# Attention, expert layer and feed-forward in one kernel: 33 slots outside any condition, one conditional block for the rest, later tile loads and decoding

## The chip, the cores and the metric

The kernel runs on one core of a Trainium2 chip. The core's engines are TensorE (PE, matrix multiplication), VectorE (DVE), ScalarE (ACT), GpSimd (POOL) and SyncE (SP, which here issues nearly all DMA). Each engine works through its own list of instructions in order and waits on semaphores for the others. The metric is the device time of one execution in microseconds (us); less is better. A measurement of this kernel can tell a change from none at about 0.3%, some 5 us.

## What is computed

Three layers follow one another on 4608 tokens of 512 values.

```python
x = attention(q, k, v, phi)                  # 8 batches x 8 heads, 576 positions, 64 values a head
idx = argmax(logits(x, expert_emb)); gate = softmax(...)[idx]
for e in range(8):                           # each token goes to one of 8 experts
    out[idx == e] = gate * (relu(x[idx == e] @ w1[e]) @ w2[e])      # 512 -> 1024 -> 512
h = out @ w_in                               # 512 -> 2048
y = (h * sigmoid(1.702 * h)) @ w_out         # 2048 -> 512
```

`w_in` and `w_out` come as 64-bit floats. [...] Every product is made of three 16-bit matmuls (high times high, high times low, low times high).

## The kernel before

**Expert layer.** Tokens are sorted by expert into slots of 128 rows. Four early slots run beside the end of the attention. Then `Moe.run` goes over slots 0 to 31 (`ALWAYS` = 32), which run whatever the data are. How many slots there are in all depends on the data (a table entry that `reg(2, 0)` loads into a register); with these inputs slot 32 is the last. `Moe.slot` lists the work of one slot with a time for each piece and writes it in the order of those times: the first layer of slot s (`product`, `relu`), the second layer of slot s - 1 (`second`, `measure`, `leave`), the input of slot s + 2 (`take`: scale, split, a DMA transpose into `xT`), the gather for slot s + 5, and, under a condition (`when`), the change of weights when the expert changes.

**Feed-forward.** A tile is 256 sorted tokens; there are 18. `FF` is done in two passes of 1024 hidden values, so there are 36 tile visits q, each of two halves h = 2q (first layer, line 1466, which ends in tanh and two elementwise steps) and h = 2q + 1 (second layer, line 1509). From slot 20 (`ALONE`) each slot carries one half in its middle: slot 20 + h carries half h. After the slots, `Ffn.run` does the other halves alone. `Ffn.load` brings a tile's input by SP: two DMA transposes into `x2T` (line 1447), `x2s` and `x2i`; there are two buffers. It is called in an even half, for the tile after it.

**Slots behind 31, before.** `Ffn.run` begins with half 12 and puts slot 32 and up to five more behind one half each: `swap` (weights), a conditional `alone` (the whole slot, line 1555) and `ahead` (gather and `take` of later slots, unconditional). Slots from 38 on stand in one last conditional block, `rest` (line 1561), behind half 18.

**Decoding.** `Weights.pieces` is a list of small steps; a slot or half issues some of them between its own work (`share`). The weights of the first pass are decoded in slots 0 to 18, those of the second pass from slot 20 on, 4 pieces in an even slot and 16 in the next, then 24 per tile in `Ffn.run`. The first step of a block of weights is `low`, an ACT instruction (line 1288) that reads the raw words a DMA has brought (`raw`, line 1262). `Weights.more` issues those DMAs as buffers come free. `widen` adds three more buffers in room that the dispatch tables had used, and fetches into them at once.

**Conditions.** A `tc.If` makes every engine that has work inside it load and compare the register. Where the block is skipped, the engine waits for its own earlier work and DMAs and then counts up its semaphores by what the block would have added. Whatever comes later and needs another engine's work from inside the block also waits until that engine has passed the condition.

Of the kernel before, what the change touches and what calls it, by code (L numbers as in the profile page):

```python
# [23 lines left out]
NT, DM, E, FE, FF = 4608, 512, 8, 1024, 2048  # L24
P = 128
PB = 96
NC = 6
XW = 514
YI, YS, YW = 2 * DM, 2 * DM + 2, 2 * DM + 4
HEAD = 8  # L30
EARLY = 4
ALWAYS = NT // P - EARLY
MORE = 6
ALONE = 20
HF = FF // 2
TILES = NT // (2 * P)
SHARE = 4, 16
# [10 lines left out]
def do(pieces):  # L48
    for f in pieces:
        f()  # L50
# [749 lines left out]
class Moe:  # L800
# [302 lines left out]
        if self.other:  # L1103
            self.other.pop(0)()

    def ahead(self, s):

        end = ALWAYS + MORE
        if s + 2 < end:
            do(self.take(s + 2))  # L1110
        if s + 5 < end:
            self.gather(s + 5)

    def slot(self, s, share, ffn):

        ev, end, h = [], ALWAYS + MORE, 0.65
        TR, TLO, TS, TL, TLH, TT, TG, TM, TQ, TQ1 = TIMES

        def add(t, fs, dt=0.0):
            ev.extend((t + i * dt, len(ev) + i, f) for i, f in enumerate(fs))  # L1120

        def begins(r, *fs):
            def f():
                with self.when(r):  # L1124
                    for x in fs:
                        x()
            return f

        def change(k, r):
            return lambda: self.change(k, r)  # L1130

        def bound(k):
            return lambda: self.bound(k)

        add(0, [lambda a=a, fi=fi: self.product(s, a, fi) for a in range(2) for fi in range(4)], h)
        for a in range(2):
            add(4 * h * (a + 1) + TR, self.relu(s, a), TLO)
        if s + 1 < ALWAYS:
            add(8 * h + (5 if ffn else 0), [begins(s + 1, change(0, s + 1))])
        y = 8 * h + 0.02  # L1140
        if ffn:
            add(y, ffn, 5.2)
            y += 10.4
        if s:
            add(y, [lambda k=k: self.second(s - 1, k) for k in range(8)], h)
            y += 8 * h
            m = self.measure(s - 1)
            add(y, m[:1])
            add(y, [begins(s, change(1, s))])

            add(TQ, [begins(s - 1, bound(0))] if s > 1 else [])
            add(TQ1, [begins(s - 2, bound(1))] if s > 2 else [])
        add(TM, self.later, TS)
        self.later = m[1:] if s else []
        c = self.leave(s - 2)
        add(TL, c[:1])
        add(TL + TLH, c[1:], TLO)
        if s + 2 < end:
            add(TT, self.take(s + 2), TLO)
        if s + 5 < end:  # L1160
            add(TG, [lambda: self.gather(s + 5)])
        add(0.2, share, (20 if ffn else 10.2) / max(len(share), 1))
        for _, _, f in sorted(ev, key=lambda e: e[:2]):
            f()

    def run(self, ffn):

        n, self.later = len(self.other), []
        for s in range(ALWAYS):
            left = n * (ALONE - 2 - s) // (ALONE - 1)  # L1170
            share = []
            while len(self.other) > max(left, 0):
                share.append(self.other.pop(0))
            if s == ALONE - 1:
                ffn.open()
            if s >= ALONE:
                share = ffn.share(SHARE[(s - ALONE) % 2])
            self.slot(s, share, [lambda part=part: ffn.half(s - ALONE, part) for part in range(2)] if s >= ALONE else [])
        do(self.later + self.leave(s - 1))
        self.layer2(s)  # L1180
        with self.when(s):
            self.bound(0)
            self.bound(1)
        with self.when(s - 1):
            self.bound(1)

    def layer2(self, s):
        for k in range(8):
# [22 lines left out]
    def rest(self):  # L1211

        g = self.g
        for s in range(ALWAYS + MORE, g.ns):
            with g.tc.If(self.reg(2, 0) > s):
                self.swap(s)
                self.bounds(s)
                self.gather(s)
                do(self.take(s))
                self.alone(s)  # L1220


class Weights:
# [129 lines left out]

        return [high, low]

    def pieces(self):
        n, none = self.n, [lambda: None]
        exact = self.exact
        dec = [none * 8 if exact else self.decode(k, i) for k in range(2) for i in range(n)]
        out = []  # L1360

        def at(q, j, k0, k1):
            if k0 * n <= q < k1 * n:
                out.append(dec[q][j])

        def fetch(q):
            if q < 2 * n and exact:
                out.append(lambda: self.fetch(*divmod(q, n)))

        def put(k, i, j):  # L1370
            if k and i < n:
                out.append(self.put(0, i)[j])

        fetch(0)
        fetch(1)
        out.append(self.more if not exact else lambda: None)
        at(0, 0, 0, 1)
        for k in range(2):
            if k:
                for i in range(3):  # L1380
                    for j in range(2):
                        put(k, i, j)
                at(n, 0, 1, 2)
            for i in range(n + LAG):
                q = k * n + i
                put(k, i + 3, 0)
                at(q, 1, k, k + 1)
                at(q - 1, 6, k, k + 1)
                at(q, 2, k, k + 1)
                if self.nlf > 2:  # L1390
                    at(q + 1, 0, k, k + 1)
                put(k, i + 3, 1)
                at(q, 3, k, k + 1)
                at(q - 1, 7, k, k + 1)
                if self.nlf < 3:
                    at(q + 1, 0, k, k + 1)
                at(q, 4, k, k + 1)
                at(q, 5, k, k + 1)
                if i < n:
                    fetch(q + 2)  # L1400
                w = 1024 // self.N
                if i < n and i % w == w - 1:
                    out.append(lambda k=k, j=i // w: self.square(k, j))
                if i > n:
                    out += none
            r, f = self.settle(k)
            out += none * 2 + [r] + none * 4 + [f]
        p = [self.put(1, i) for i in range(n)]
        for i in range(n + 1):
            out += ([p[i][0]] if i < n else []) + ([p[i - 1][1]] if i else [])  # L1410
        return out


class Ffn:
# [108 lines left out]
    def half(self, h, part, n=0):  # L1523

        q = h // 2
        if h % 2:
            self.layer2(q, part, n)
        else:
            if part == 0:
                if q == TILES:  # L1530
                    self.factors(1)
                if q + 1 < 2 * TILES:
                    self.load(q + 1)
            elif q >= TILES:
                self.room2(q)
            self.layer1(q, range(4 * part, 4 * part + 4))
            if part:
                self.after(self.x[q], 0)

    def run(self):  # L1540

        g, moe = self.g, self.moe
        s, end = ALWAYS, ALWAYS + MORE
        moe.swap(s)
        for h in range(ALWAYS - ALONE, 4 * TILES):
            if h == 2 * TILES:
                do(self.share(len(self.other)))
            for part in range(2):
                self.half(h, part, 3)
            if h == ALWAYS - ALONE:  # L1550
                do(moe.leave(ALWAYS - 1))
            if ALWAYS < s <= end:
                moe.bounds(s - 1)
            if s < end:
                with g.tc.If(moe.reg(2, 0) > s):
                    moe.alone(s)
                if s + 1 < end:
                    moe.swap(s + 1)
                moe.ahead(s)
            elif s == end:  # L1560
                with g.tc.If(moe.reg(2, 0) > s):  # L1561
                    moe.rest()
            s += 1


@with_exitstack
def tile_kernel(ctx, tc, q, k, v, phi, emb, tau, w1, w2, w_in, w_out, out):
    nc = tc.nc
    g = Obj()
# [23 lines left out]
    moe = Moe(g, ctx.enter_context(tc.tile_pool(name="w", bufs=1)))  # L1593
    g.xp = ctx.enter_context(tc.tile_pool(name="xp", bufs=1))
    g.psa = ctx.enter_context(tc.tile_pool(name="psa", bufs=1, space=PSUM))
    with tc.manual_schedule():
        at, aq, wst, wsr = ExitStack(), ExitStack(), ExitStack(), ExitStack()
# [18 lines left out]

        attention(g, moe, second)
        at.close()
        g.weights.widen(wsr.enter_context(tc.tile_pool(name="wsr", bufs=1, side="right", reuse_waits="tile")))

        def third():
            wsr.close()
            wst.close()
            g.fp = ctx.enter_context(tc.tile_pool(name="fp", bufs=2, reuse_waits="tile"))
            p = ctx.enter_context(tc.tile_pool(name="wst2", bufs=1, reuse_waits="tile"))
            return Weights(g, 1, p, moe.junk, DM // 2, 2).pieces()

        ffn = Ffn(g, moe, third)
        moe.run(ffn)
# [31 lines left out]
```

## Time and profile before

| what | value |
|---|---|
| time, median of 3 runs (lowest, highest) | 1538.82 us (1536.34, 1541.42) |
| time of the profiled execution | 1532.62 us |
| its span, first to last instruction | 1530.7 us |
| PE busy | 1373.3 us, 90% |
| DVE busy | 886.1 us, 58% |
| ACT busy | 697.7 us, 46% |
| POOL busy | 274.8 us, 18% |
| mean granted TensorE clock | 0.952 of full speed |

The profiled execution took 1.92 us more than its span. Busy times are sums over the whole span; where an engine waited has to be read from stretches of it.

### The profile page before, as it was taken

How to read it: one execution, taken by the hardware profiler on the slowest of the kernel's cores; microseconds unless marked ns; L12 is line 12 of the kernel's file. 1: busy time of each engine (PE TensorE's matmuls, PEld its weight loads, DVE VectorE, ACT ScalarE, POOL GpSimd, SP SyncE). 2: the span in 40 equal slices, each digit the busy share in tenths (PEclk: the TensorE clock that was granted, in tenths of full speed). 3: DMA queues.
4: the chain of work that ended last, by engine and by line, in shares of the span. 5: the costliest groups of instructions: out<-in, count | busy, mean ns of one | idle time of the engine just before them, and what ended most of it. 6: DMA issues, size and time to landing. Idle time of an engine off the chain costs nothing. (4 is left out here: it accounts for less than half of the span.)

```text
span 1530.7 us, 31869 instructions
## 1 busy us (share of the span) xinstructions
PE 1373.3 (90%) x11632; PEld 963.4 (63%) x11632; DVE 886.1 (58%) x2232; ACT 697.7 (46%) x1655; POOL 274.8 (18%) x301
## 2 busy tenths in 40 slices
PE   4989877878789886989999988899999999999997
PEld 4767656556557555666667645566666666666664
DVE  3887995866456543465564455676545554445553
ACT  2767864444645542355564344354533332223331
POOL 2543430442122210111011011111000011110011
PEclk9987888989899998999999999999999999999999
DMA  9999933798785875564343454233214323333321
GB/s 214 240 231 260 248 88 96 171 169 145 117 92 96 137 63 93 87 155 99 74 67 88 74 82 89 60 95 77 53 51 105 83 75 89 77 83 90 84 73 42
DMA packets 229809, 168.87 MB, mean 110 GB/s; under 512 B 149338, under 2 KB 199130, under 8 KB 229602
## 3 DMA queue, kind: packets, MB, share of 16 engines
q1 hardware_dynamic: 223362, 145.85, 46.0%
q0 software_dynamic: 6240, 20.50, 6.8%
q8 instruction: 101, 1.65, 0.6%
q14 instruction: 106, 0.87, 0.4%
HBM read 96.60 MB, written 39.82 MB: 89 GB/s over the span
## 5 line engine op out<-in xcount | busy, mean ns | idle before, releaser
L1509 PE MATMUL op<-wo,gt 128*128 128x512 f16 x1728 | 386.2, 383 | 18.3 <-DVEq L1561 5.9
L1466 PE MATMUL hp<-x2T,wi 128*128 128x256 f16 x3456 | 387.1, 274 | 17.2 <-DVE th L1480 12.1
L1466 PEld LDWEIGHTS <-wi 128*128 128x128 f16 x3456 | 338.6, 98 | 66.5 <-issue 20.0
L1509 PEld LDWEIGHTS <-gt 128*128 128x128 f16 x1728 | 170.3, 99 | 220.3 <-issue 16.7
L1471 ACT ACTIVATE th<-th,fk 128x256 f32<-128x256 f32 x288 | 145.9, 508 | 342.0 <-DVE th L1470 340.7
L985 PE MATMUL hp<-xT,wh 128*128 128x128 f16 x3552 | 214.1, 223 | 32.3 <-ACTq L1124 9.1
L985 PEld LDWEIGHTS <-wh 128*128 128x128 f16 x3552 | 208.2, 100 | 46.7 <-issue 32.3
L1010 PE MATMUL yp<-wh,hT 128*128 128x512 f16 x888 | 204.7, 388 | 14.4 <-PEq L1124 8.0
L1470 DVE TENSOR_TENSOR th<-hp,x2s 128x256 f32<-128x256 f32 x288 | 122.1, 424 | 157.1 <-PE hp L1466 152.9
L1010 PEld LDWEIGHTS <-hT 128*128 128x128 f16 x888 | 86.9, 100 | 120.5 <-PEq L1124 12.7
L1480 DVE SCALAR_TENSOR_TENSOR th<-th,hp 128x256 f32<-128x256 f32 x288 | 118.7, 412 | 16.5 <-ACT th L1471 16.4
L1490 DVE SCALAR_TENSOR_TENSOR gt<-th,gt 128x256 f16<-128x256 f32 x288 | 121.1, 420 | 6.3 <-ACT gt L1482 3.5
L1482 ACT ACTIVATE gt<-th 128x256 f16<-128x256 f32 x288 | 115.9, 402 | 7.8 <-DVE th L1480 7.5
L1516 POOL DMA_INDIRECT out_dram<-o,x2i x36 | 35.4, 984 | 427.2 <-DVE o L1515 427.2
L1515 DVE SCALAR_TENSOR_TENSOR o<-op,x2f,o 128x512 f32<-128x512 f32 x36 | 27.0, 751 | 126.3 <-PE op L1509 126.3
L1309 POOL TENSOR_TENSOR dlf<-dlf,raw 128x256 f32<-128x256 f32 (+1 forms) x48 | 46.5, 970 | 240.3 <-DVE raw L1305 101.6
L1001 DVE SCALAR_TENSOR_TENSOR hT<-hp,hT 128x512 f16<-128x512 f32 x74 | 50.7, 687 | 66.1 <-ACT hT L998 47.4
L956 POOL DMA_INDIRECT xg<-xbuf,idx x38 | 40.0, 1052 | 272.6 <-DVE hT L1001 135.1
L1520 ACT ACTIVATE o<-op,x2f 128x512 f32<-128x512 f32 x36 | 24.7, 686 | 112.9 <-PE op L1509 111.7
L370 PE MATMUL xp<-bdv,aT 128*96 128x264 f32 x192 | 65.9, 454 | 9.7 <-ACT xh L376 4.9
L998 ACT ACTIVATE hT<-hp 128x512 f16<-128x512 f32 x74 | 43.5, 589 | 61.1 <-PE hp L985 59.7
L971 DVE SCALAR_TENSOR_TENSOR x<-xg,x 128x512 f16<-128x512 f32 x42 | 37.7, 898 | 50.3 <-ACT x L966 48.7
(250 smaller groups left out, 1460.2 us busy)
## 6 DMA issues: line engine op xcount, KB each, us to landing
wr<-in_moe_w_dram SPq DMA_DIRECT2D x40, 512.0 KB
xbuf<-xh SPq DMA_DIRECT2D x18, 576.0 KB
yb<-y SPq DMA_DIRECT2D x37, 257.0 KB
qr<-in_q_dram SPq DMA_DIRECT2D x16, 576.0 KB
kv<-in_k_dram SPq DMA_DIRECT2D x16, 576.0 KB
kv<-in_v_dram SPq DMA_DIRECT2D x16, 576.0 KB
part<-o SPq DMA_DIRECT2D x36, 256.0 KB
o<-part SPq DMA_DIRECT2D x36, 256.0 KB
```

The source lines that it names most:

```text
L370: nc.tensor.matmul(t[:PB], lhsT=self.aT[:, c], rhs=self.bdv, start=True, stop=True)
L985: self.g.nc.tensor.matmul(o.hp[a][:, fi], lhsT=self.wh[0][f // 2][:, ta, k, f % 2 * P:f % 2 * P + P], rhs=o.xT[:, 4 * tb + k], start=(n == ...
L1001: nc.vector.scalar_tensor_tensor(out=part(1), in0=o.hp[a], scalar=0.0, in1=part(0), op0=ALU.max, op1=ALU.subtract)
L1010: self.g.nc.tensor.matmul(o.yp, lhsT=o.hT[:, ta, k], rhs=self.wh[1][k // 2][:, tb, k % 2], start=(k + i == 0), stop=(k + i == 9))
L1309: nc.gpsimd.tensor_tensor(out=o.lf, in0=o.lf, in1=o.lo.bitcast(F32), op=ALU.mult)
L1466: nc.tensor.matmul(x.hp, lhsT=w.wi[:, ta, k, a * P:(a + 1) * P], rhs=o.xT[:, 4 * tb + k].rearrange("p j q -> p (j q)"), start=(i == 0), st ...
L1470: nc.vector.tensor_tensor(out=x.th, in0=x.hp, in1=o.s, op=ALU.mult)
L1471: nc.scalar.activation(out=x.th, in_=x.th, func=AF.Tanh, scale=k2[:, 0:1])
L1480: nc.vector.scalar_tensor_tensor(out=x.th, in0=x.th, scalar=1.0, in1=x.hp, op0=ALU.add, op1=ALU.mult)
L1482: nc.scalar.activation(out=o.gt[-1][:, 0], in_=x.th, func=AF.Copy, scale=2.0**-GS)
L1490: self.g.nc.vector.scalar_tensor_tensor(out=o.gt[i][:, 1], in0=o.th[i], scalar=2.0**-GS, in1=o.gt[i][:, 0], op0=ALU.mult, op1=ALU.subtract)
L1509: nc.tensor.matmul(op, lhsT=o.gt[a][:, ta, j * P:(j + 1) * P], rhs=w.wo[:, a, tb], start=(i == 0), stop=(i == 23))
```

## The change

- `ALWAYS` is 33, so slot 32 is written like the slots ahead of it and carries half 12. `Ffn.run` begins with half 13. `ahead` and the five conditional slots behind single halves are gone, and so are their unconditional gathers and `take`s.
- All slots from 33 on stand in one condition, `rest`, which is issued in half 13 between its two parts. The conditional `bound`s that ended `Moe.run` go into it.
- `Ffn.load(q + 1)` is no longer in half 2q, in the middle of slot 20 + 2q, but at the head of slot 21 + 2q. The tile is used in half 2q + 2 as before.
- In the second pass 20 empty pieces stand behind the first fetch. With 4 and 16 pieces a slot, decoding starts in slot 22 and not in slot 20.
- `widen` is called in slot 1, at time 6 of the slot's list, and not ahead of slot 0.

```diff
 NC = 6
 XW = 514
 YI, YS, YW = 2 * DM, 2 * DM + 2, 2 * DM + 4
+WIDE = 1
 HEAD = 8
 EARLY = 4
-ALWAYS = NT // P - EARLY
-MORE = 6
+ALWAYS = NT // P - EARLY + 1
 ALONE = 20
 HF = FF // 2
 TILES = NT // (2 * P)
...
         if self.other:
             self.other.pop(0)()

-    def ahead(self, s):
-
-        end = ALWAYS + MORE
-        if s + 2 < end:
-            do(self.take(s + 2))
-        if s + 5 < end:
-            self.gather(s + 5)
-
     def slot(self, s, share, ffn):

-        ev, end, h = [], ALWAYS + MORE, 0.65
+        ev, end, h = [], ALWAYS, 0.65
         TR, TLO, TS, TL, TLH, TT, TG, TM, TQ, TQ1 = TIMES

         def add(t, fs, dt=0.0):
...
             add(TT, self.take(s + 2), TLO)
         if s + 5 < end:
             add(TG, [lambda: self.gather(s + 5)])
+        if s == WIDE:
+            add(6, [self.widen])
         add(0.2, share, (20 if ffn else 10.2) / max(len(share), 1))
         for _, _, f in sorted(ev, key=lambda e: e[:2]):
             f()
...
                 ffn.open()
             if s >= ALONE:
                 share = ffn.share(SHARE[(s - ALONE) % 2])
+
+                if (s - ALONE) % 2:
+                    ffn.load((s - ALONE) // 2 + 1)
             self.slot(s, share, [lambda part=part: ffn.half(s - ALONE, part) for part in range(2)] if s >= ALONE else [])
         do(self.later + self.leave(s - 1))
         self.layer2(s)
-        with self.when(s):
-            self.bound(0)
-            self.bound(1)
-        with self.when(s - 1):
-            self.bound(1)

     def layer2(self, s):
         for k in range(8):
...
     def rest(self):

         g = self.g
-        for s in range(ALWAYS + MORE, g.ns):
-            with g.tc.If(self.reg(2, 0) > s):
-                self.swap(s)
-                self.bounds(s)
-                self.gather(s)
-                do(self.take(s))
-                self.alone(s)
+        self.reg(2, 0)
+        with g.tc.If(self.reg(2, 0) > ALWAYS):
+            with self.when(ALWAYS - 1):
+                self.bound(0)
+                self.bound(1)
+            with self.when(ALWAYS - 2):
+                self.bound(1)
+            for s in range(ALWAYS, g.ns):
+                with g.tc.If(self.reg(2, 0) > s):
+                    self.swap(s)
+                    self.bounds(s)
+                    self.gather(s)
+                    do(self.take(s))
+                    self.alone(s)


 class Weights:
...

         return [high, low]

-    def pieces(self):
+    def pieces(self, wait=0):
+
         n, none = self.n, [lambda: None]
         exact = self.exact
         dec = [none * 8 if exact else self.decode(k, i) for k in range(2) for i in range(n)]
...
         fetch(0)
         fetch(1)
         out.append(self.more if not exact else lambda: None)
+        out += wait * none
         at(0, 0, 0, 1)
         for k in range(2):
             if k:
...
             if part == 0:
                 if q == TILES:
                     self.factors(1)
-                if q + 1 < 2 * TILES:
+                if ALWAYS - ALONE <= h and q + 1 < 2 * TILES:
                     self.load(q + 1)
             elif q >= TILES:
                 self.room2(q)
...

     def run(self):

-        g, moe = self.g, self.moe
-        s, end = ALWAYS, ALWAYS + MORE
-        moe.swap(s)
-        for h in range(ALWAYS - ALONE, 4 * TILES):
+        moe, first = self.moe, ALWAYS - ALONE
+        for h in range(first, 4 * TILES):
             if h == 2 * TILES:
                 do(self.share(len(self.other)))
             for part in range(2):
+                if h == first and part == 0:
+                    self.load(h // 2 + 1)
                 self.half(h, part, 3)
-            if h == ALWAYS - ALONE:
-                do(moe.leave(ALWAYS - 1))
-            if ALWAYS < s <= end:
-                moe.bounds(s - 1)
-            if s < end:
-                with g.tc.If(moe.reg(2, 0) > s):
-                    moe.alone(s)
-                if s + 1 < end:
-                    moe.swap(s + 1)
-                moe.ahead(s)
-            elif s == end:
-                with g.tc.If(moe.reg(2, 0) > s):
+                if h == first and part == 0:
+                    do(moe.leave(ALWAYS - 1))
                     moe.rest()
-            s += 1


 @with_exitstack
...

         attention(g, moe, second)
         at.close()
-        g.weights.widen(wsr.enter_context(tc.tile_pool(name="wsr", bufs=1, side="right", reuse_waits="tile")))
+        wide = wsr.enter_context(tc.tile_pool(name="wsr", bufs=1, side="right", reuse_waits="tile"))
+        moe.widen = lambda: g.weights.widen(wide)

         def third():
             wsr.close()
             wst.close()
             g.fp = ctx.enter_context(tc.tile_pool(name="fp", bufs=2, reuse_waits="tile"))
             p = ctx.enter_context(tc.tile_pool(name="wst2", bufs=1, reuse_waits="tile"))
-            return Weights(g, 1, p, moe.junk, DM // 2, 2).pieces()
+            return Weights(g, 1, p, moe.junk, DM // 2, 2).pieces(sum(SHARE))

         ffn = Ffn(g, moe, third)
         moe.run(ffn)
```

The order of ACT's list in slot 20 before: `relu` of the slot (`hT`), then the first decoding step of the second pass (`dlf<-raw`), then the tanh (`th`) and gate (`gt`) steps of half 0.

```order
L1124 UNCONDITIONAL_BRANCH x2
L998 ACTIVATE hT<-hp 128x512
L1288 ACTIVATE dlf<-raw 128x256
L1471 ACTIVATE th<-th,fk 128x256 x2
L1482 ACTIVATE gt<-th 128x256
L1471 ACTIVATE th<-th,fk 128x256
```

And now, at the same place:

```order
L1116 UNCONDITIONAL_BRANCH x2
L998 ACTIVATE hT<-hp 128x512
L1472 ACTIVATE th<-th,fk 128x256 x2
L1483 ACTIVATE gt<-th 128x256
L1472 ACTIVATE th<-th,fk 128x256
L1483 ACTIVATE gt<-th 128x256
```

The instruction that reads `raw` has left slot 20; it stands in the same way ahead of the tanh steps of half 2, in slot 22.

SP's list now, from the end of slot 20 into slot 21: the skipped fetch of an expert's second weights (`wr`), the load of tile 1, a condition, a partial result (`part`) and the `xT` of a later slot.

```order
L846 DMA wr_142<-in_moe_w_dram 128x2x512
L920 UNCONDITIONAL_BRANCH x2
L1116 UNCONDITIONAL_BRANCH
L1448 DMA_TRANSPOSE x2T<-yb 128x8x128 x2
L1451 DMA x2s<-ys 128x256
L1453 DMA x2i<-yb 128x2x4
L1116 COMPARE_AND_BRANCH
L1116 UNCONDITIONAL_BRANCH x2
L1522 DMA part<-o 128x512
L973 DMA_TRANSPOSE xT<-x_9155 128x8x128
```

Before, the load of tile 1 stood in slot 20 itself, directly behind the three fetches of `raw` and one condition; the load has moved behind slot 20's writes of `yb` and `ys`.

DVE's list now, in half 13 between its parts: decoding steps, the two instructions that end slot 32 (`y`), then the load of the register and the condition at line 1207.

```order
L1301 SCALAR_TENSOR_TENSOR wo_3030<-raw,wo_3030 128x256
L1304 TENSOR_SCALAR raw<-wo_3030 128x256
L1290 TENSOR_SCALAR wo_3030<-raw 128x256
L1044 TENSOR_TENSOR y_13235<-ym,fac 128x1
L1050 SCALAR_TENSOR_TENSOR y_13235<-yp,yr,y_13235 128x512
L838 TENSOR_LOAD tabs
L1207 COMPARE_AND_BRANCH
L1208 COMPARE_AND_BRANCH
```

Before, the last such condition (line 1561) stood behind the last gate step of half 18; now it stands behind slot 32's last output, and behind it on TensorE comes the second part of half 13.

## Rows read from the trace of the kernel before

**Rows 1.** The page's DMA issues: names, engine, operation, count, size.
```profile
yb<-y SPq DMA_DIRECT2D x37, 257.0 KB
```

**Rows 2.** Windows: stretch, length, busy time (instructions) of each engine, granted clock, DMA share, GB/s.
```profile
573.22:609.95 36.73, 24.19 (x216) 18.38 (x217) 12.90 (x35) 10.35 (x26) 1.35 (x3) 0.81 0.60 97
...
833.76:979.28 145.52, 127.92 (x890) 80.08 (x891) 75.01 (x203) 56.22 (x131) 17.45 (x25) 0.94 0.42 75
979.28:1519.00 539.72, 539.72 (x3737) 365.57 (x3736) 289.55 (x762) 199.08 (x469) 49.06 (x55) 1.00 0.31 77
```

**Rows 3.** Timeline of PE in slot 20: start, duration, work, [idle before, what ended it].
```profile
573.22 5.52 PE L985 MATMUL hp<-xT,wh 128*128 128x128 f16 x96
578.84 5.41 PE L1466 MATMUL hp<-x2T,wi 128*128 128x256 f16 x48
596.35 8.08 PE L1466 MATMUL hp<-x2T,wi 128*128 128x256 f16 x48 [12.09 <-DVE th L1480]
...
609.95 2.23 PE L985 MATMUL hp<-xT,wh 128*128 128x128 f16 x37 [0.35 <-PEq L1124]
```

**Rows 4.** Timeline of ACT in slot 20.
```profile
595.01 0.43 ACT L1288 ACTIVATE dlf<-raw 128x256 f32<-128x256 uint32 x1 [18.31 <-DMA raw<-in_moe_w_in_dram]
```

**Rows 5.** Timeline of SP's DMA issues, end of slot 19 and slot 20.
```profile
572.97 3.80 SPq L1447 DMA_TRANSPOSE x2T<-yb  x2
...
584.36 1.29 SPq L1262 DMA_DIRECT2D raw<-in_moe_w_in_dram  x3
585.95 10.22 SPq L1447 DMA_TRANSPOSE x2T<-yb  x2
```

**Rows 6.** Timeline of PE: the starts of slots 26, 27 and 28.
```profile
723.24 5.52 PE L985 MATMUL hp<-xT,wh 128*128 128x128 f16 x96
...
745.13 5.52 PE L985 MATMUL hp<-xT,wh 128*128 128x128 f16 x96 [0.39 <-DVE raw L1305]
...
767.27 4.91 PE L985 MATMUL hp<-xT,wh 128*128 128x128 f16 x85
```

**Rows 7.** Timeline of PE from slot 31 to half 20.
```profile
833.76 5.52 PE L985 MATMUL hp<-xT,wh 128*128 128x128 f16 x96 [0.30 <-DVE th L1470]
...
855.88 5.34 PE L1010 MATMUL yp<-wh,hT 128*128 128x512 f16 x24 [1.06 <-ACTq L1124]
...
885.56 9.40 PE L1509 MATMUL op<-wo,gt 128*128 128x512 f16 x36 [2.99 <-ACT x L966]
...
911.86 12.21 PE L1509 MATMUL op<-wo,gt 128*128 128x512 f16 x48 [2.54 <-DVEq L1555]
...
967.42 12.02 PE L1509 MATMUL op<-wo,gt 128*128 128x512 f16 x48 [5.93 <-DVEq L1561]
979.28 10.64 PE L1466 MATMUL hp<-x2T,wi 128*128 128x256 f16 x96
```

**Rows 8.** Source view of line 1561: count, duration ns min/median/max, first and last start.
```profile
L1561 PEldq COMPARE_BRANCH x1: 3802/3802/3802, 959.6 to 959.6; - x1
```

**Rows 9.** Source view of line 1555, the same columns.
```profile
L1555 PEldq COMPARE_BRANCH x7: 70/342/570, 870.6 to 946.9; - x7
```

**Rows 10.** Timeline of DVE behind the condition at line 1561.
```profile
967.49 0.23 DVE L1504 TENSOR_SCALAR x2f<-x2i,fk 128x2 f32<-128x2 f32 x1 [3.57 <-DVEq L1561]
```

**Rows 11.** Timeline of ACT and DVE in slot 21: one tile output, one slot output.
```profile
620.69 0.69 ACT L1520 ACTIVATE o<-op,x2f 128x512 f32<-128x512 f32 x1 [7.26 <-PE op L1509]
...
622.46 0.69 ACT L1047 ACTIVATE y<-yp,yr 128x512 f16<-128x512 f32 x1
623.82 0.75 DVE L1050 SCALAR_TENSOR_TENSOR y<-yp,yr,y 128x512 f16<-128x512 f32 x1
```

**Rows 12.** Timeline of PE, ACT and SP in slots 0 and 1.
```profile
319.49 0.39 PE L985 MATMUL hp<-xT,wh 128*128 128x128 f16 x2 [8.69 <-ACTq L1124]
318.24 0.66 ACT L1288 ACTIVATE dlf<-raw 128x512 f32<-128x512 uint32 x1 [8.28 <-SPq L1124]
307.42 6.23 SPq L1262 DMA_DIRECT2D raw<-in_moe_w_in_dram  x4
```

## The prediction

> **What bounds the kernel now.** I read the windows first, then the timeline of PE in the two stretches that the diff touches, then who ended its waits. The chain of work that ended last shows only the final output transfers, so it does not help. From 979.28 us on PE is busy all the time at a granted clock of 1.00 [rows 2]: 52 halves in 539.72 us, 10.38 us a half. That stretch is bound by matmuls, and the diff adds and removes none there. So the end moves by what the start of half 20 moves, and that is decided ahead of it.
>
> Two stretches ahead of it lose time. [...] The stretch from slot 31 to half 20 takes 145.52 us with PE busy 127.92, clock 0.94 [rows 2]. A slot with a half in it that meets no such wait takes 745.13 - 723.24 = 21.89 us (slot 26, even) or 767.27 - 745.13 = 22.14 us (slot 27, odd) [rows 6].
>
> In slot 20 PE stands idle 12.09 us until DVE's `th` step [rows 3]. DVE is only the last link: ACT is in order, and ahead of its tanh stands the first decoding step, which waited 18.31 us for `raw` to land [rows 4]. SP issued those three fetches at 584.36 and tile 1's transposes right behind them; the latter took 10.22 us to issue, against 3.80 us for tile 0's [rows 5]. From first issue to use a fetch took 595.01 - 584.36 = 10.65 us. So a fetch is read as soon as it can be, with a tile load crowding it, on the one engine that half 0 needs.
>
> From slot 31 to half 20 the waits end on conditions and on the `take` of slots that never run: 2.99 us (ACT's `x`, line 966), 2.54 (line 1555), 5.93 (line 1561) [rows 7]. The 37 writes of `yb` are 4 early slots and slots 0 to 32 [rows 1]: slot 32 runs, and no later one does.
>
> **Slot 20.** With 20 empty pieces, 4 + 16, ACT reads `raw` in slot 22, some 44 us (two slots) after the fetch; the longest latency above is 10.65 us. The tile load no longer crowds it either. Slot 20 becomes an even slot like slot 26: 36.73 - 21.89 = 14.8 us saved. Lower bound: only the idle time goes, 12.1. Where could the stall go? The same decoding step now stands ahead of slot 22's tanh, but its data are old by then. In `Ffn.run` decoding is 16 pieces further behind: 365 pieces with the empty ones, less 124 issued in slots 20 to 32, leaves 241, and the 12 odd halves 13 to 35 take 24 each, 288. So nothing is left to be dumped at half 36. Cost there: nothing, hidden by PE, which is busy all that time while DVE is busy 289.55 of 539.72 us [rows 2].
>
> **Tile loads.** In program order `load(q + 1)` comes later, not sooner: from the middle of an even slot to the head of the next odd one. Four DMAs move past SP's `xT` and `yb` of the even slot and ahead of `part` and `xT` of the odd one. The room left is one odd slot and the first product of the next, 22.14 + 5.52 = 27.7 us. Tile 0's load was used 578.84 - 572.97 = 5.9 us after its first issue, without a wait [rows 3, 5]; the crowded one needed at least its 10.22 us. Both fit. Behind the moved issues (about 5 us of SP's time) wait `part` and an `xT` that is used two slots later. I take 0.
>
> **Slots 31 and 32, halves 12 to 19.** Now: slot 31, 22.14; slot 32 with half 12, 21.89; slot 32's second layer, 5.34 plus the 1.06 us that it waits for a condition on ACT, as slot 31's does at 855.88 [rows 7], 6.40; halves 13 to 19, 7 x 10.38 = 72.66. That is 123.1 us before the one condition that remains.
>
> That condition (line 1207) stands between the parts of half 13. TensorE's second part needs a PSUM buffer that the block's last slot would use, so it waits until DVE has passed the condition. From the end of the first part: ACT writes `o`, 0.69; ACT writes `y`, 0.69; DVE writes `y`, 0.75 [rows 11]; the register's load, which no row shows alone, for which I take the 0.34 us median of a short conditional step [rows 9]; DVE's idle time over such a condition, 3.57 [rows 10]: 6.0 us together. The old one cost PE 5.93 [rows 7]. PE's own 3.80 us over it [rows 8] runs beside that. After the old wait half 19 took 979.28 - 967.42 = 11.86 instead of 10.38 us, 1.5 for the lower clock; I take that again. Sum: 123.1 + 6.0 + 1.5 = 130.6, against 145.52: 14.9 us saved. Bounds of the wait: 3.8 (PE's own) and twice 6.0, if the skip also has to wait for SP's two writes of slot 32, which stand just ahead of it; behind SP's condition are two `raw` fetches, a `part` and tile 8, all used a half or more later.
>
> Here length could matter, since the block holds 17 slots and the old one 12. The conditions around one slot (line 1555) took PE 0.07 to 0.57 us, the one around 12 slots 3.80 [rows 8, 9]: a jump over much code costs more than one over little, but two points don't tell how it grows. If DVE's 3.57 grew with length it would be 3.57 x 17/12 = 5.06, and the whole 1.5 us dearer. [...] I stay at 6.0.
>
> **`widen`.** PE waits 8.69 us in slot 0 for ACT, and ACT 8.28 for a `raw` that it decodes [rows 12]. SP's four fetches around 307.42 to 313.65 hold that one and two of the three that `widen` adds behind it. The one that ACT waits for is issued first in either order, so removing later fetches should change nothing: 0. Bounds: the three crowd it, and all 8.7 us go; or the three, now ahead of slot 3's `xT`, delay it by up to the 10.65 us of a fetch. ACT decodes in the same order as before.
>
> **Sum.** 14.8 + 14.9 = 29.7 us. The profiled execution took 1532.62 us, 1.92 more than its span; its span becomes 1530.7 - 29.7 = 1501.0 and its time 1502.9. The median of the runs shown is 1538.82, 6.2 us above the profiled one, so on that footing I forecast 1538.82 - 29.7 = 1509 us, a ratio of 0.981.
>
> **Rivals.**
> - Slot 0's wait goes as well. For it: several transfers share the time in which ACT waits. Against it: the order of issue. 1509 - 8.7 = 1500.
> - The condition costs double, 6 us more, through SP's fresh writes: 1515.
> - The change doesn't do what it says in slot 20: the decoding step waits again in slot 22, because its fetch waits for room or is crowded by tile 2. For it: the same step on the same engine. Against it: two slots of slack. 14.8 us come back: 1524.
> - On the other side: the tile arrives late. If a load at the head of an odd slot lands only after the even slot's first product, each of the six even slots 22 to 32 waits, and PE can do nothing else, as its list is in order. Price 6 times the wait; from 29.7 / 6 = 5.0 us a slot on, the kernel is slower than before. A load would have to take 27.7 + 5.0 = 33 us; at 7 us a slot the time is 1551. Against it: 5.9 and some 10 us [rows 3, 5].
>
> **How the numbers follow.** The forecast 0.75, slot 0's wait gone too 0.08, the dearer condition 0.06, slot 22 waits 0.06, late tiles 0.05. The time is that of the first, 1509. Its own uncertainty: 12.1 instead of 14.8 in slot 20, 3.8 to 7.5 instead of 6.0 at the condition, about 3 us, and some 5 between sets of runs. The range 1498 to 1521 takes in the first three cases and a little of the fourth. A measurement of this kernel can tell a difference of about 0.3%, 5 us; all cases but the last are faster by more, and a few shares of late tiles lie about zero: faster 0.93, within 0.3% 0.03, slower 0.04.
>
> **What would show it.** In the profile after: slot 20 about 22 us long, its clock 1.00, and no wait of ACT's decoding step for `raw` in slots 20 to 22; no wait of PE at lines of single conditional slots; one PE wait near 6 us inside half 13, ended by DVE at the condition, and a slow part behind it; slot 31 to half 20 about 131 us; tile transposes landed before each first product of line 1467; slot 0 as before; then 52 halves at 10.38 us. I am wrong if PE waits for `x2T`, for `raw` in slot 22, or if the wait in half 13 is well over 10 us.

## The result, and the profile after

The changed kernel took 1522.05 us (median of 11 runs, 1514.12 to 1531.22), the kernel before 1538.82 (11 runs, 1533.42 to 1550.27): a ratio of 0.9883, 95% interval 0.9851 to 0.9916. It is 16.8 us faster where 29.7 were forecast, and the median lies 1 us above the upper end of the range. By the ratio to the kernel before it is 0.9883 x 1538.82 = 1520.8, just inside. The profiled execution took 1528.7 us, span 1527.0.

The windows of the changed kernel, cut at the starts of the slots: slots 0 to 3, slots 4 to 19, slot 20, slots 21 to 30, slot 31 to half 20, and the rest (stretch, length, busy time of PE, PEld, DVE, ACT, POOL with instructions, granted clock, DMA share, GB/s).

```profile
307.38:367.18 59.80, 42.09 (x458) 32.10 (x457) 33.69 (x60) 21.12 (x46) 19.82 (x19) 0.86 0.89 128
367.18:589.24 222.06, 186.67 (x1933) 131.91 (x1933) 121.13 (x248) 110.00 (x211) 47.91 (x52) 0.93 0.77 107
589.24:611.19 21.95, 21.50 (x216) 16.94 (x217) 12.09 (x32) 10.06 (x25) 1.46 (x3) 1.00 0.72 102
611.19:841.95 230.76, 216.24 (x1928) 148.94 (x1929) 117.08 (x294) 111.31 (x231) 23.54 (x37) 0.99 0.55 90
841.95:975.92 133.97, 123.37 (x891) 79.39 (x892) 69.18 (x200) 52.64 (x122) 16.53 (x25) 0.96 0.38 75
975.92:1527.00 551.08, 542.14 (x3747) 366.46 (x3745) 293.93 (x773) 200.59 (x472) 51.10 (x58) 0.99 0.30 77
```

Both stretches on which the sum was built became shorter: slot 20 from 36.73 to 21.95 us at a clock of 1.00, slot 31 to half 20 from 145.52 to 133.97 [rows 2]. The tail from half 20 on stayed: 551.08 now, 1530.7 - 979.28 = 551.4 before. But slot 20 begins at 589.24, against 573.22 before [rows 3]. The rest of this section shows the two stretches and then the place where time went.

PE in slot 20 (start, duration, work, [idle before, what ended it]), to be held against [rows 3]; and below it the first decoding step of the second pass on ACT (decoding is the rebuilding of the 64-bit weights from the two 32-bit words of each number):

```profile
589.24 5.52 PE L985 MATMUL hp<-xT,wh 128*128 128x128 f16 x96
594.75 5.41 PE L1467 MATMUL hp<-x2T,wi 128*128 128x256 f16 x48
600.31 5.40 PE L1467 MATMUL hp<-x2T,wi 128*128 128x256 f16 x48
605.55 5.34 PE L1010 MATMUL yp<-wh,hT 128*128 128x512 f16 x24
```
```profile
636.71 0.43 ACT L1287 ACTIVATE dlf<-raw 128x256 f32<-128x256 uint32 x1
```

The 12.09 us ahead of the second part are gone. The decoding step stands in slot 22 and has no bracket: it waited for nothing, where it waited 18.31 us before [rows 4].

PE from slot 31 to half 20, answering to [rows 7]:

```profile
841.95 5.52 PE L985 MATMUL hp<-xT,wh 128*128 128x128 f16 x96 [0.30 <-DVE th L1471]
...
886.28 5.34 PE L1010 MATMUL yp<-wh,hT 128*128 128x512 f16 x24 [1.00 <-ACTq L1116]
891.46 5.34 PE L1510 MATMUL op<-wo,gt 128*128 128x512 f16 x24
905.17 7.68 PE L1510 MATMUL op<-wo,gt 128*128 128x512 f16 x24 [8.37 <-DVEq L1207]
912.69 10.64 PE L1467 MATMUL hp<-x2T,wi 128*128 128x256 f16 x96
```

The waits at single conditional slots are gone, and one long wait is left, inside half 13, ended by DVE at the block's condition. It is 8.37 us long (forecast 6.0), and the part behind it runs 7.68 us in place of 5.34.

Where time went: slots 0 to 3 take 59.80 us, against 356.92 - 305.28 = 51.64 before. PE from slot 2 to slot 3, and SP's DMA issues ahead of slot 3; behind them the product of slot 3 and the issue of its `xT` in the kernel before:

```profile
341.68 5.34 PE L1010 MATMUL yp<-wh,hT 128*128 128x512 f16 x24 [0.30 <-PEq L1116]
352.17 7.79 PE L985 MATMUL hp<-xT,wh 128*128 128x128 f16 x96 [5.15 <-DMA xT<-x]
361.69 5.34 PE L1010 MATMUL yp<-wh,hT 128*128 128x512 f16 x24 [1.73 <-PEq L1116]
```
```profile
332.10 0.35 SPq L1261 DMA_DIRECT2D raw<-in_moe_w_in_dram  x1
332.50 0.90 SPq L1261 DMA_DIRECT2D raw<-in_moe_w_out_dram  x2
333.54 11.74 SPq L973 DMA_TRANSPOSE xT<-x  x1
345.38 0.52 SPq L1261 DMA_DIRECT2D raw<-in_moe_w_out_dram  x1
```
```profile
345.61 5.52 PE L985 MATMUL hp<-xT,wh 128*128 128x128 f16 x96
331.21 1.26 SPq L973 DMA_TRANSPOSE xT<-x  x1
```

The three `raw` fetches that `widen` adds stand directly ahead of slot 3's `xT`. Its issue takes 11.74 us (1.26 before), PE waits 5.15 for it (before, not at all), and the product that follows takes 7.79 us instead of 5.52, at a granted clock of 0.69 over these 7.79 us. That is the upper bound that the prediction named for `widen` and did not take. Slots 21 to 30 are longer too, 230.76 against 223.81, so two places are open: is the loss of slots 0 to 3 a property of the new order or chance, and does another part of the change cost something in slots 4 to 30?

### The profile page after: what moved, and what is told of

Same layout as the page of the kernel before. It is cut to its first block, busy times and chain, and to the rows that moved or that the text cites. A ratio compares the mean times of both kernels' runs of the same rounds, so it can differ in the third digit from the quotient of the medians.

```text
span 1527.0 us, 31624 instructions
## 1 busy us (share of the span) xinstructions
PE 1375.2 (90%) x11632; PEld 970.0 (64%) x11632; DVE 879.4 (58%) x2227; ACT 693.5 (45%) x1645; POOL 269.6 (18%) x296
## 5 line engine op out<-in xcount | busy, mean ns | idle before, releaser
L985 PE MATMUL hp<-xT,wh 128*128 128x128 f16 x3552 | 218.5, 225 | 39.8 <-DMA xT<-x 17.4
L985 PEld LDWEIGHTS <-wh 128*128 128x128 f16 x3552 | 212.3, 101 | 53.8 <-issue 36.5
L1010 PE MATMUL yp<-wh,hT 128*128 128x512 f16 x888 | 202.0, 384 | 17.8 <-DVE y L1044 5.6
L1001 DVE SCALAR_TENSOR_TENSOR hT<-hp,hT 128x512 f16<-128x512 f32 x74 | 50.8, 687 | 80.0 <-ACT hT L998 50.8
L956 POOL DMA_INDIRECT xg<-xbuf,idx x33 | 34.7, 1052 | 204.1 <-DVE hT L1001 83.8
L1521 ACT ACTIVATE o<-op,x2f 128x512 f32<-128x512 f32 x36 | 24.6, 685 | 99.8 <-PE op L1510 98.6
L850 ACT ACTIVATE wjunk<-wr 128x1024 bf16<-128x1024 f32 x48 | 50.5, 1053 | 26.3 <-SPq L1116 24.6
```

Source lines behind the costliest of these rows:

```text
L850: self.g.nc.scalar.activation(out=self.junk, in_=flat(self.raws[k][i]), func=AF.Square, accum_out=self.m[:, k, i:i + 1])
L985: self.g.nc.tensor.matmul(o.hp[a][:, fi], lhsT=self.wh[0][f // 2][:, ta, k, f % 2 * P:f % 2 * P + P], rhs=o.xT[:, 4 * tb + k], start=(n == ...
L1001: nc.vector.scalar_tensor_tensor(out=part(1), in0=o.hp[a], scalar=0.0, in1=part(0), op0=ALU.max, op1=ALU.subtract)
L1010: self.g.nc.tensor.matmul(o.yp, lhsT=o.hT[:, ta, k], rhs=self.wh[1][k // 2][:, tb, k % 2], start=(k + i == 0), stop=(k + i == 9))
```

## The experiments

Theory: the parts gain what was forecast in slot 20 and from slot 31 on, and `widen` in slot 1 takes some of it back through SP's order. Rivals: the loss is chance, or it lies in the tile loads, the later decoding, or the block's longer wait. Three sets of four kernels were run, each set on one chip with the kernel before beside it; the three sets were on different chips. Times are compared inside a set.

### First set: the parts added one after another

Decoding alone (the kernel before with this):

```diff
         out.append(self.more if not exact else lambda: None)
+        out += wait * none
         at(0, 0, 0, 1)
...
-            return Weights(g, 1, p, moe.junk, DM // 2, 2).pieces()
+            return Weights(g, 1, p, moe.junk, DM // 2, 2).pieces(sum(SHARE))
```

> The kernel before with one part of the change: decoding of the second pass two slots later. Theory 1 (the steps of the prediction hold and widen was mis-sized): slot 20 falls from 36.7 to about 22 us, nothing waits for raw in slot 22, the whole is 14.8 us faster, ratio to before 0.990. Rival (the stall moves: the tile load, still in slot 20, or the later decoding crowd something else): 5 us or less faster, ratio 0.997 or more.

Decoding and block. Against the changed kernel the loads and `widen` are put back:

```diff
-                if (s - ALONE) % 2:
-                    ffn.load((s - ALONE) // 2 + 1)
...
-        if s == WIDE:
-            add(6, [self.widen])
...
-                if ALWAYS - ALONE <= h and q + 1 < 2 * TILES:
+                if q + 1 < 2 * TILES:
...
-                if h == first and part == 0:
-                    self.load(h // 2 + 1)
...
-        moe.widen = lambda: g.weights.widen(wide)
+        g.weights.widen(wide)
```

> The kernel before with two parts: decoding two slots later, and 33 slots always run with one block behind them. Loads and widen as before. Theory 1: the block adds a gain of 11.6 us, which is what the stretch from slot 31 to half 20 lost in the two profiles (145.52 to 133.97); together 26.4 us faster, ratio 0.983. Rival (the longer wait in half 13 and its slow clock are dearer over many runs): the block adds 5 us or less, ratio 0.987 or more.

Decoding, block and loads: only the two `widen` places of that diff are put back.

> Three parts: decoding, block, and loads at the head of odd slots; only widen stands as before, ahead of slot 0. It is the changed kernel with widen undone. Theory 1: the loads add nothing and widen's new place costs 9 us (slot 3 waits 5.15 us for xT, then 1.73 us, and runs 2.3 us slower), so this one is 9 us faster than the changed kernel: ratio to before 0.983, and no wait for xT in slot 3. Rival (what is missing went into the loads: slots 21 to 30 were 7.0 us longer in the changed kernel's profile, and the stretch ahead of slot 20 differs by chance): this one is as slow as the changed kernel, ratio 0.988, and 7 us slower than the kernel with two parts.

All four parts, the changed kernel unaltered:

> The changed kernel once more, all four parts, beside the other steps. Theory 1: ratio 0.988, 9 us behind the kernel without the widen part, with the wait for xT in slot 3 again, since it follows from the order of SP's list. Rival (that wait was chance): it is gone or elsewhere in this profile, and the ratio is that of the kernel with widen undone.

| first set | median us | against before | ratio, 95% interval |
|---|---|---|---|
| before (17 runs) | 1516.34 | | |
| decoding (12 runs) | 1505.37 | -11.0 | 0.9931, 0.9905 to 0.9956 |
| decoding, block (6) | 1493.72 | -22.6 | 0.9857, 0.9817 to 0.9896 |
| decoding, block, loads (6) | 1491.70 | -24.6 | 0.9860, 0.9822 to 0.9899 |
| all four (6) | 1494.26 | -22.1 | 0.9857, 0.9824 to 0.9890 |

Decoding and block each gain: decoding 11.0 us, less than the 14.8 expected and more than its rival's 5, and the block 11.6 more, as expected. The loads cost nothing that can be measured. The `widen` part cost 2.6 us by the medians, where 9 were expected, although its trace shows the stall at the same place as before:

```profile
349.89 7.14 PE L985 MATMUL hp<-xT,wh 128*128 128x128 f16 x96 [3.59 <-DMA xT<-x]
```

The execution traced here was the longest of its six, 1508.70 us, so the stall's local price and the medians had to be told apart by a second set.

### Second set: the kernel before again, `widen` again, four more empty pieces

> The kernel before once more, for a second trace of it. If what the change gained less than forecast lies in slots 0 to 19 (theory 2), this trace has slots 0 to 19 in about 250 us, as the three traces with the old widen (249.8 to 252.6). If those traces were only taken on a chip that is faster there (theory 1: the change does nothing ahead of slot 20 except through widen), it is 250 as well; if instead decoding, block or loads had gained something ahead of slot 20, it stays near the 268 of the first trace. Slot 20 should be 36.7 long, slots 21 to 30 223.8, slot 31 to half 20 145.5.

> Decoding, block and loads, with widen as before (the same kernel as the three parts above), to measure widen against the next one again. Theory 1 (the order of SP's list delays slot 3's xT in every execution): 9 us or more faster than the kernel with all parts, and slots 0 to 19 about 250 us. Theory 2 (widen's place makes stalls only in some executions, and its mean price is small, as the medians of 1491.7 and 1494.3 say): at most 4 us faster.

> All four parts again, third trace. Theory 1: the wait for xT in slot 3, 3 to 5 us, stands in this trace too, slots 0 to 19 take about 270 us, and the median is 9 us or more above the one with widen as before. Theory 2: the trace has that wait or not, the median is within 4 us.

The fourth kernel is decoding, block and loads, `widen` as before, and one line more:

```diff
-            return Weights(g, 1, p, moe.junk, DM // 2, 2).pieces(sum(SHARE))
+            return Weights(g, 1, p, moe.junk, DM // 2, 2).pieces(sum(SHARE) + 4)
```

> Decoding, block and loads, widen as before, and 24 empty pieces in place of 20. In all traces with 20 the sum of squares of the decoded weights (ACT, line 1317 to 1320, 1.25 us), which ran in slot 27 before, runs in slot 29 right behind the four of the expert's weights and ahead of ACT's o; TensorE waits 2.91 us there in place of 1.05 and then runs one part at the lower clock. Four pieces later it comes behind o. Theory 1 (that is the 2.5 us by which slots 21 to 30 grew): the wait is 1.05 again, slots 21 to 30 take 224 us, the whole is 2 to 3 us faster than with 20. Rival (the growth comes from SP's loads or from the later fetches): the wait stays near 2.9, or slots 21 to 30 stay at 226.

| second set | median us | against before | ratio, 95% interval |
|---|---|---|---|
| before (11 runs) | 1529.60 | | |
| before, one traced run | 1540.89 | | |
| decoding, block, loads (6) | 1504.27 | -25.3 | 0.9823, 0.9783 to 0.9863 |
| all four (6) | 1516.22 | -13.4 | 0.9900, 0.9856 to 0.9943 |
| three parts, 24 pieces (6) | 1502.50 | -27.1 | 0.9803, 0.9760 to 0.9847 |

Here `widen` in slot 1 cost 12.0 us. So neither of the two sentences about it held as written: it is not 9 in every set, and not at most 4.

The new trace of before has slots 0 to 19 at 266 us, like the first. By its expectation that would mean that the other parts gained something there. They did not: with `widen` put back the same chip took 271.6 us for these slots. Slots 4 to 19 vary between sets and executions, from 200.8 to 222.1 us over all traces, and that inference falls.

The 24 pieces were meant for a wait in slot 29. ACT there with 20 empty pieces (second kernel of this set): the last sum of squares of the expert's weights (`wr`), one of the decoded weights (`wo`, line 1317), `hT`, and then the tile output `o` for which PE waits.

```profile
782.07 1.06 ACT L850 ACTIVATE wjunk<-wr 128x1024 bf16<-128x1024 f32 x1
783.03 0.18 ACT L850 ACTIVATION_READ_ACCUMULATOR wjunk<-wr 128x1 f32 x1
783.25 1.06 ACT L1317 ACTIVATE wjunk<-wo 128x1024 bf16<-128x1024 f32 x1
784.21 0.19 ACT L1317 ACTIVATION_READ_ACCUMULATOR wjunk<-wo 128x1 f32 x1
784.30 0.58 ACT L998 ACTIVATE hT<-hp 128x512 f16<-128x512 f32 x1
786.10 0.69 ACT L1519 ACTIVATE o<-op,x2f 128x512 f32<-128x512 f32 x1 [1.22 <-issue]
```

PE waits for that `o` first with 20 and then with 24 pieces, in the two kernels:

```profile
786.84 5.34 PE L1508 MATMUL op<-wo,gt 128*128 128x512 f16 x24 [2.92 <-ACT o L1519]
```
```profile
789.66 5.34 PE L1508 MATMUL op<-wo,gt 128*128 128x512 f16 x24 [1.71 <-ACT o L1519]
```

In the two traces of before it is 1.05 and 0.78 us. With 24 pieces the sum of squares does come behind `o`, but another decoding step has moved to where it was, directly ahead of `hT`:

```profile
786.80 0.42 ACT L1285 ACTIVATE dlf<-raw 128x256 f32<-128x256 uint32 x1
```

So the wait shrinks, but not to 1.05. The mechanism holds, the price does not: slots 21 to 30 take 224.43 us with 20 and 225.05 with 24 pieces, and the medians differ by 1.8 us, less than a measurement tells. They took 223.81 and 227.42 in the two traces of before, so the 7.0 us of the first comparison were not shown to be an effect of the change.

### Third set: where the fetches stand, and the block's price

> All four parts, as the reference of the next run, fourth trace. Expected from the three traces so far: from slot 0's first product to slot 4's 54.6 to 59.8 us, with a wait for xT of 3 to 5 us in slot 3; the six traces with widen ahead of slot 0 took 48.6 to 52.6.

> Decoding, block and loads, widen ahead of slot 0, as the reference of the next two. Expected: slots 0 to 3 in 48.6 to 52.6 us, no wait for xT in slot 3, and a median 2 to 12 us below the kernel with all parts, as in the two sets before.

The next kernel has all four parts, with `widen` still in slot 1 but behind the `take`:

```diff
         if s == WIDE:
-            add(6, [self.widen])
+            add(TT + TLO, [self.widen])
```

> All four parts, but widen in slot 1 is called right behind the take, so that on SP slot 3's xT stands ahead of the first of the fetches in place of behind three of them; nothing else in SP's list differs. Theory 1 (xT waits because plain fetches are ahead of it in SP's list): the wait for xT in slot 3 is gone, slots 0 to 3 take 49 to 53 us, and the median is that of widen ahead of slot 0. Rival (widen in slot 1 is dear because the three buffers are filled later, whatever the order, and decoding on ACT and DVE lags): slots 0 to 3 still take 55 us or more, the median is that of all four parts.

The last one has decoding, block and loads, with `widen` ahead of slot 0, and leaves out the conditional block for slots from 33 on (with these inputs no such slot runs):

```diff
                 if h == first and part == 0:
                     do(moe.leave(ALWAYS - 1))
-                    moe.rest()
```

> Decoding, block and loads, widen ahead of slot 0, and the conditional block for slots from 33 on left out altogether (with these inputs it is skipped; with others they would be missing). Theory 1 (the wait in half 13 and the slow clock behind it are its whole price): TensorE doesn't wait in half 13, slot 31 to half 20 falls from 131.5 to 123 us, the sum of slots and halves without condition in the prediction, and the whole is 7 to 9 us faster than with the block. Rival (the conditions also hide work that would be waited for otherwise, SP's and decoding's): 4 us or less.

| third set | median us | against before | ratio, 95% interval |
|---|---|---|---|
| before (14 runs) | 1529.13 | | |
| all four (9) | 1516.86 | -12.3 | 0.9905, 0.9872 to 0.9938 |
| decoding, block, loads (6) | 1504.55 | -24.6 | 0.9825, 0.9787 to 0.9863 |
| all four, `widen` behind `xT` (6) | 1509.42 | -19.7 | 0.9860, 0.9825 to 0.9895 |
| three parts, no block (6) | 1500.33 | -28.8 | 0.9797, 0.9755 to 0.9839 |

SP and then PE with `widen` behind the `take`, and below them the same transpose and product in this set's all-four kernel:

```profile
331.74 1.26 SPq L973 DMA_TRANSPOSE xT<-x  x1
333.05 0.56 SPq L1261 DMA_DIRECT2D raw<-in_moe_w_in_dram  x1
333.66 3.71 SPq L1261 DMA_DIRECT2D raw<-in_moe_w_out_dram  x3
```
```profile
345.46 5.52 PE L985 MATMUL hp<-xT,wh 128*128 128x128 f16 x96 [0.15 <-PEq L1116]
353.44 5.34 PE L1010 MATMUL yp<-wh,hT 128*128 128x512 f16 x24 [2.46 <-PEq L1116]
```
```profile
335.09 10.24 SPq L973 DMA_TRANSPOSE xT<-x  x1
352.64 8.28 PE L985 MATMUL hp<-xT,wh 128*128 128x128 f16 x96 [4.18 <-DMA xT<-x]
```

With the same fetches behind it, `xT` is issued in 1.26 us and PE does not wait for it; in this set's all-four kernel the issue took 10.24 us and PE waited 4.18. So the order on SP is the cause of that wait. It gives back 7.4 of the 12.3 us between the first two kernels of the set; in slot 3 PE then waits 2.46 us at a condition on its weights, where the all-four kernel waited 1.23. Both theories are partly right: slots 0 to 3 take 53.61 us, near the 49 to 53 expected, but the median is not that of `widen` ahead of slot 0. The remaining 4.9 us are about the least that a measurement can tell; if they are real they belong to the later place, and their mechanism is open.

PE and SP behind half 13 without the block:

```profile
871.17 10.52 PE L1508 MATMUL op<-wo,gt 128*128 128x512 f16 x48
883.48 10.65 PE L1465 MATMUL hp<-x2T,wi 128*128 128x256 f16 x96 [1.78 <-DMA x2T<-yb]
```
```profile
878.59 2.65 SPq L1446 DMA_TRANSPOSE x2T<-yb  x2
```

There is no wait in half 13, but half 14 waits 1.78 us for its tile, and half 15 waits 1.25 us for ACT's sum of squares of the decoded weights:

```profile
899.26 0.38 PE L1325 MATMUL fr<-fs,ones 128*128 128x4 f32 x2 [1.25 <-ACT wjunk L1317]
```

The traces with the block show neither, so its wait had covered both. Slot 31 to half 20 takes 125.99 us in this one trace, against 130.67 to 133.57 in the five with the block (133.57 in this set). The forecast's bare sum of 123.1 us lacked that cover. So the block costs 5 to 8 us in its stretch, less than its wait of 7.31 us in this set and the slow part behind it (8.05 us in place of 5.34), because other things would be waited for next. The median is 4.2 us lower, which a measurement of this kernel can just not tell from none.

Lengths in us from the starts of the slots' first products on PE, over all traces:

| kernels | slots 0-3 | slots 4-19 | slot 20 | slots 21-30 | slot 31 to half 20 |
|---|---|---|---|---|---|
| before (2 traces) | 51.64, 50.31 | 216.30, 215.90 | 36.73, 36.31 | 223.81, 227.42 | 145.52, 145.24 |
| decoding alone (1) | 48.56 | 201.27 | 21.79 | 225.99 | 147.39 |
| `widen` as before, with block (5) | 49.97 to 52.54 | 200.83 to 221.01 | 21.79 | 224.43 to 226.66 | 130.67 to 133.57 |
| the same, no block (1) | 52.35 | 213.38 | 21.79 | 226.17 | 125.99 |
| all four (4) | 54.56 to 59.80 | 215.46 to 222.06 | 21.79 to 22.39 | 224.48 to 230.76 | 131.36 to 133.97 |
| `widen` behind `xT` (1) | 53.61 | 216.33 | 23.37 | 227.37 | 131.87 |

## Why the prediction was right in direction and too large

**Slot 20: right, and shown.** 21.79 to 22.39 us in all traces with the changed decoding, forecast 21.89, but for 23.37 with `widen` behind `xT`, where PE waited 1.40 us for tile 0. Decoding alone does it. In slot 22 nothing waits for `raw`, so that rival is out.

**Slot 31 to half 20: right within 2 us, and shown.** The mean with the block is 132.2 us over ten traces (forecast 130.6), 146.1 over the three traces with the old arrangement: 13.9 saved, forecast 14.9. The wait in half 13 was 4.79 to 8.37 us, mean 6.65, for 6.0. That it takes the place of the waits spread over halves 13 to 19 held; the doubled wait (rival two) was not seen.

**The length of the block.** PE's own step over the block took longer now than over the shorter one before (here its second trace):

```profile
L1207 PEldq COMPARE_BRANCH x1: 5966/5966/5966, 893.2 to 893.2; - x1
```
```profile
L1561 PEldq COMPARE_BRANCH x1: 3553/3553/3553, 968.0 to 968.0; - x1
```

The three traces with 12 slots in the block show 3.37, 3.55 and 3.80 us [rows 8], four with 17 slots 5.22, 5.33, 5.97 and 6.12. The prediction stayed at 6.0 us for the longer block as well; that the longer skip costs no more was shown by no run, and these steps of PE do not agree with it. The blocks also stand in different surroundings, so growth with length is likely but not shown. On DVE, which the forecast was about, the idle time behind the condition was 3.23, 3.50 and 3.57 us over 12 slots [rows 10] and 2.9, 4.1, 5.0 and 6.43 over 17 in those four traces: the two groups overlap. For the sum it was little: PE waits for DVE there, in the mean of ten traces 6.65 us for the 6.0 forecast.

**Tile loads: right.** Adding them moved the median by -2.0 us, inside the intervals, and the changed kernel's trace shows no wait for `x2T`. The rival on the other side, late tiles in six slots, did not occur. Slot 29's longer wait for `o`, by 1.9 to 2.1 us, is a stall that the later decoding made elsewhere; the prediction asked what is late next and looked only at the same step in slot 22. With decoding alone, a wait at a single conditional slot (line 1556) was also 4.23 us, against 2.54 before, and slot 31 to half 20 took 147.39 us, against 145.24 and 145.52.

**`widen`: the step that failed.** The prediction took 0 between -8.7 and +10.65. It watched slot 0, where indeed nothing changed (PE waited 9.18 us, 8.69 before), and gave the other bound no rival. Yet its own rows held the pattern: in slot 20 two tile transposes right behind three fetches of `raw` took 10.22 us to issue, against 3.80 [rows 5]. Slots 0 to 3 take 57.8 us in the mean of four traces with `widen` in slot 1 and 50.8 in the mean of nine with it ahead of slot 0; the two groups do not overlap. That is +7.0 us. The whole cost 2.6, 12.0 and 12.3 us in the three sets. The error was in the reason given: that later fetches can change nothing is true of the fetch ahead of them, not of a transpose behind them.

**The sum.** The mean of slot 20 fell by 14.7 us (36.52 to 21.86, without the 23.37). 14.7 + 13.9 - 7.0 = 21.6 us by the traces; the four measurements of the whole give 16.8, 22.1, 13.4 and 12.3. Without the `widen` part the traces give 28.6, the medians 24.6, 25.3 and 24.6. Some 3 to 4 us that slot 20 and the block save are thus not seen at the end, already with decoding alone (11.0 for 14.7, where the interval ends at 14.4). The intervals of the second and third set still hold 28.6, that of the first does not, and stretches in which nothing of these parts stands vary by more: slots 4 to 19 by 20 us between traces, and slot 0 begins between 301.49 and 312.31 us. Where the 3 to 4 us are stays open. Whether `widen`'s later place also costs something in slots 4 to 19 is not settled: the five traces with it in slot 1 took 215.46 to 222.06 us there, the seven with the changed decoding and `widen` ahead of slot 0 200.83 to 221.01.

The kernel with decoding, block, loads and `widen` ahead of slot 0 beats the kernel before, with ratios of 0.982 to 0.986 in three sets. It is 12 us ahead of the changed kernel in two of them; in the first the 2.6 us between the two are within the noise.

## What to carry to other kernels

When fetches are moved on an in-order DMA issuer, look first at what they now stand ahead of, and give the bound that hurts a chance of its own; here one transpose behind three plain fetches cost 7.0 us in its stretch, about a quarter of the forecast gain. Moving a stalled consumer far behind its fetch, and gathering conditions that are never taken into one, gave what the rows promised in their own stretches. A part that gains locally should be checked over several executions: waits elsewhere varied by more than the part that was lost.

## What the runs showed of the hardware

- Slot 3's `xT` transpose, placed behind three plain fetches on SP, held the queue 11.74, 11.42 and 10.24 us in three of four traces (in the fourth no `xT` took more than 3.73 to issue, and PE still waited 3.59); ahead of the same fetches it took 1.26. Not every transpose behind a fetch was slow: in the trace of the kernel before, one at 376.97 us right behind a single fetch took 1.28 us. Why these were slow is open.
- Kernels with `widen` ahead of slot 0 took 200.8 to 202.0 us for slots 4 to 19 in the first set and 210.5 to 221.0 in the other two; the longest wait for `xT` in each of these traces was 3.2 to 7.1 us. The kernel before had medians from 1516.34 to 1538.82 us over the four measurements.
- Skipping a block is not free, and the price is not constant: over the same 17 slots PE's own step took 5.22 to 6.12 us in four traces, and DVE, for which PE had to wait, stood idle 2.9 to 6.43 us behind the condition; over 12 slots it was 3.37 to 3.80 and 3.23 to 3.57 us in three traces [rows 8, 10].
